# Expert 0's first two inner chunks in pieces of 192 and 96 tokens, and 28 stand-ins behind a branch, in a fused attention and mixture-of-experts kernel

## The chip, the cores and the metric

The kernel runs on one core of a Trainium2 chip. The metric is the device time of one execution in microseconds (us), the median of the runs made. A core has five engines that work side by side, each through its own queue in order: TensorE (PE in the profile, PEld for its weight loads), VectorE (DVE), ScalarE (ACT), GpSimd (POOL) and SyncE (SP, which here only issues DMAs).

## The reference

Attention over a window of 128 keys with a bias by distance, for 4 batches, 8 heads and 576 positions of width 64; then a first layer of 8 experts, to which the 2304 tokens are dealt out by the order of their gate logits, 288 to each; then a dense second layer. Cut to the two layers:

```python
flat = (x @ w_gate).flatten()
order = np.argsort(-flat)               # tokens to experts, 288 at most for each
...
for e in range(E):
    mask = assigned == e
    h = np.maximum(x[mask] @ w1[e], 0.0)   # 288 x 512 by 512 x 1024
    out[mask] = h @ w2[e]
...
h = x @ w_in
return (h * (1.0 / (1.0 + np.exp(-h)))) @ w_out
```

## The kernel before

Four stages follow one another on the core: attention tile by tile (to some 120 us), the routing that turns logits into a list of tokens for each expert (to 140 us), the first layer expert by expert (`moe1`, to some 370 us), and the second layer in groups of 512 tokens (`moe2`, to the end). Products of float32 are made as three matmuls of rounded parts: each operand x is split into a high part `xh` (a cast) and the rest `xl` (a subtraction), and hi*xh, lo*xh and hi*xl are summed in PSUM. Weights are split in the same way (`Weights.fetch`: a DMA into `raw`, a cast on ScalarE, line 728, and a subtraction on VectorE, line 729). Three weights of the first layer are split during attention, in `split_early`; the others follow on the run.

Between routing and the first layer stands a branch (line 1024): if the fast routing did not deal out all tokens properly, a slow one is run. With these inputs it is not taken into that code. Ahead of it, `gather0` (line 1021) has POOL issue three indirect DMAs that fetch expert 0's 288 tokens as three tiles of 96 into `xg0`, which lies in a buffer of the weights' ring. Behind it TensorE runs stand-ins (`k.busy`, line 440: matmuls on constants whose result is not read; here 256 columns each, into the PSUM tile `pd`), as many as the first number of `BUSY_G` says.

`gather(e)` in `moe1` makes `xh` and `xl` of an expert: for each tile of 96 tokens four transposes on TensorE (line 836) into PSUM, a cast on ScalarE (line 843) and a subtraction on VectorE (line 844). For expert 0 further stand-ins come behind the transposes of each tile, and the third tile goes through two PSUM tiles (`y2`, `y3`) in two halves. For the other experts POOL issues the gathers (line 825).

`first(e, f)` makes chunk f (128 of 1024 inner columns) of an expert: 12 matmuls (line 859) of 128x128 by 128x288, then the ReLU's high part on ScalarE (line 862) and its rest on VectorE (line 863). `second(e, f)` adds 12 further matmuls (lines 758 to 760). For each chunk the loop calls `first`, then `fetch` of the weight four chunks ahead, and `second` two chunks later. The order of instructions within an engine is chosen by a planner from estimated times, but not between those marked with `keep_in_program_order`: these stay in the order of the program. An engine's queue is served in its order, so an instruction that waits holds all behind it.

The PSUM pool `ph` has two buffers: `pd` takes one, and chunks' results `p` take turns. `px` (two) holds the transposes of a tile, `py` the four sums of `second`.

Of the kernel before, what the change touches and what calls it, by code (L numbers as in the profile page):

```python
# [8 lines left out]
F32 = mybir.dt.float32  # L9
F32R = mybir.dt.float32r  # L10
# [4 lines left out]
ALU = mybir.AluOpType  # L15
# [4 lines left out]
P = 128  # L20
B, H, S, D = 4, 8, 576, 64
# [3 lines left out]
CAP = N // E  # L25
# [367 lines left out]
JR = 96  # L393
JT = N // JR
PER = CAP // JR
# [288 lines left out]
DC = 4  # L684
# [72 lines left out]
def three(nc, out, whi, wlo, xhi, xlo, start, stop):  # L757
    nc.tensor.matmul(out, whi, xhi, start=start, stop=False)  # L758
    nc.tensor.matmul(out, whi, xlo, start=False, stop=False)  # L759
    nc.tensor.matmul(out, wlo, xhi, start=False, stop=stop)  # L760
# [5 lines left out]

SOON = 7
LATE = (0, 1, 2, 4, 5, 7, 8, 10, 11)
BUSY_G = (12, 4, 4, 3)


def load_group(tc, pool, yd, g, width=BT):

    o, n = GROUPS[g]
    r = pool.tile([P, DC, width], F32, name="yr", bufs=1)
    tc.nc.sync.dma_start(r[:, :, :n], yd.rearrange("c p n -> p c n")[:, :, o:o + n])
    return r


def split_group(tc, pool, r, g, y=None, cols=range(DC)):  # L780
    o, n = GROUPS[g]
    yh, yl = y or (pool.tile([P, DC, BT], F32R, name=x, bufs=1)[:, :, :n] for x in ("yh", "yl"))
    for c in cols:
        i = tc.nc.scalar.copy(yh[:, c], r[:, c, :n])
        j = tc.nc.vector.tensor_tensor(yl[:, c], r[:, c, :n], yh[:, c], ALU.subtract)
        if len(cols) < DC:
            tc.keep_in_program_order(i)
            tc.keep_in_program_order(j)
    return yh, yl


def moe(tc, wts, xtab, xg0, idx96, k, yd, yg, by128, idx128, out):
    nc = tc.nc
    with tc.tile_pool(name="ph", bufs=2, space=PSUM) as ph, tc.tile_pool(name="py", bufs=1, space=PSUM) as py, \
            tc.tile_pool(name="px", bufs=2, space=PSUM) as px:
        y0, p0 = moe1(tc, wts, xtab, xg0, idx96, k, yd, yg, by128, ph, py, px)
        moe2(tc, wts, yd, yg, y0, p0, idx128, out, ph, py, px)


def part0(tc, wts, p, yh, yl, f):  # L800

    hi, lo = wts.ready[E * FC1 + f]
    for dc in range(DC):
        w = slice(dc * P, dc * P + P)
        three(tc.nc, p, hi[:, w], lo[:, w], yh[:, dc, :], yl[:, dc, :], dc == 0, dc == DC - 1)


def moe1(tc, wts, xtab, xg0, idx96, k, yd, yg, by128, ph, py, px):

    nc = tc.nc  # L810
    with tc.tile_pool(name="m1", bufs=2) as m1:
        xs = {}
        ident = k.ident
        pd = ph.tile([P, CAP], F32, name="p")
        k.busy(tc, pd, BUSY_G[0], 2)

        def gather(e):
            xh = m1.tile([P, DC, CAP], F32R, name="xh")
            xl = m1.tile([P, DC, CAP], F32R, name="xl")
            for j in range(PER):  # L820
                if e == 0:
                    xg = xg0[0:JR, j]
                else:
                    xg = m1.tile([JR, H * D], F32, name="xg", bufs=3)
                    nc.gpsimd.indirect_dma_start(xg, None, xtab,
                                                 bass.IndirectOffsetOnAxis(ap=idx96[:, e * PER + j:e * PER + j + 1], axis=0))
                halves = (slice(0, 2), slice(2, 4)) if e == 0 and j == PER - 1 else (slice(0, 4),)
                pts = []
                for i, d in enumerate(halves):
                    if len(halves) == 1:  # L830
                        pt = px.tile([P, DC, JR], F32, name="pt")
                    else:
                        pt = py.tile([P, 512], F32, name=f"y{2 + i}")[:, 0:DC * JR].rearrange("p (a b) -> p a b", b=JR)
                    pts.append(pt)
                    for dc in range(d.start, d.stop):
                        tr = nc.tensor.transpose(pt[:, dc, :], xg[:, dc * P:dc * P + P], ident[0:JR, 0:JR])  # L836
                        if e < 2:
                            tc.keep_in_program_order(tr)
                if e == 0:
                    k.busy(tc, pd, BUSY_G[j + 1], 2)  # L840
                for d, pt in zip(halves, pts):
                    c = slice(j * JR, (j + 1) * JR)
                    x = nc.scalar.copy(xh[:, d, c], pt[:, d])  # L843
                    y = nc.vector.tensor_tensor(xl[:, d, c], pt[:, d], xh[:, d, c], ALU.subtract)
                    if e == 0:
                        tc.keep_in_program_order(x)
                        tc.keep_in_program_order(y)
            xs[e] = (xh, xl)

        def first(e, f):  # L850
            xh, xl = xs[e]
            hi, lo = wts.ready[e * FC1 + f]
            p = ph.tile([P, CAP], F32, name="p")

            steps = [(w, x, dc) for w, x in ((hi, xh), (lo, xh), (hi, xl)) for dc in range(DC)]
            if e + f == 0:
                steps = [(w, xh, dc) for dc in range(DC) for w in (hi, lo)] + steps[8:]
            for i, (w, x, dc) in enumerate(steps):
                nc.tensor.matmul(p, w[:, dc * P:dc * P + P], x[:, dc, :], start=(i == 0), stop=(i == 11))  # L859
            hh = m1.tile([P, CAP], F32R, name="hh", bufs=3)  # L860
            hl = m1.tile([P, CAP], F32R, name="hl", bufs=3)
            nc.scalar.activation(hh, p, AF.Relu)
            nc.vector.scalar_tensor_tensor(hl, p, 0.0, hh, ALU.max, ALU.subtract)
            return hh, hl

        ys = {}

        def second(e, f, h):
            hh, hl = h
            hi, lo = wts.ready.pop(e * FC1 + f)  # L870
            if f == 0:
                ys[e] = [py.tile([P, 512], F32, name=f"y{d}")[:, 0:CAP] for d in range(DC)]
            for d in range(DC):
                w = slice(512 + d * P, 512 + d * P + P)
                three(nc, ys[e][d], hi[:, w], lo[:, w], hh, hl, f == 0, f == FC1 - 1)
            if f == FC1 - 1:
                yo = m1.tile([P, DC, CAP], F32, name="yo", bufs=1)
                for d in range(DC):
                    nc.scalar.copy(yo[:, d], ys[e][d])
                nc.sync.dma_start(yd.rearrange("c p n -> p c n")[:, :, e * CAP:(e + 1) * CAP], yo)  # L880

        gather(0)
        wts.fetch(5)
        pend, y0 = [], None
        for e in range(E):
            for f in range(FC1):
                n = e * FC1 + f
                h = first(e, f)
                wts.fetch(n + 4)
                if n % 9 == 4 and n // 9 < SOON:  # L890
                    wts.fetch64(n // 9, wts.keep)
                if f == 3 and e == 2:
                    by128(px.tile([P, 3, JT // 4], F32, name="pt"))
                if f == 1 and e + 1 < E:
                    gather(e + 1)
                pend.append((e, f, h))
                if len(pend) > 2:
                    second(*pend.pop(0))
                if e == E - 1 and f == 1:
                    r0 = load_group(tc, yg, yd, 0)  # L900
                if e == E - 1 and 2 < f < 7:
                    y0 = split_group(tc, yg, r0, 0, y0, (f - 3,))
        second(*pend.pop(0))
        p0 = px.tile([P, BT], F32, name="pt")
        part0(tc, wts, p0, *y0, 0)
        second(*pend.pop(0))
    return y0, p0
# [177 lines left out]
```

## Time and profile before

| | us |
|---|---|
| timed runs | 760.45, 762.08, 762.80 (median 762.08) |
| profiled execution | 764.28 |
| its span, from the first to the last instruction | 762.5 |
| TensorE busy in the span | 745.0 |
| VectorE, ScalarE, POOL busy | 423.5, 328.9, 120.7 |
| granted TensorE clock, mean | 0.994 |

The profiled execution is one execution by itself, 1.5 to 3.8 us longer than the timed ones. All times of rows are counted from the start of its span. A granted clock of 1.00 is 2.4 GHz, 0.50 is 1.2 GHz. Busy time of matmuls is modelled from their starts, and matmuls overlap, so that the distance from start to start tells their pace.

### The profile page before, as it was taken

How to read it: one execution, taken by the hardware profiler on the slowest of the kernel's cores; microseconds unless marked ns; L12 is line 12 of the kernel's file. 1: busy time of each engine (PE TensorE's matmuls, PEld its weight loads, DVE VectorE, ACT ScalarE, POOL GpSimd, SP SyncE). 2: the span in 40 equal slices, each digit the busy share in tenths (PEclk: the TensorE clock that was granted, in tenths of full speed). 3: DMA queues.
4: the chain of work that ended last, by engine and by line, in shares of the span. 5: the costliest groups of instructions: out<-in, count | busy, mean ns of one | idle time of the engine just before them, and what ended most of it. 6: DMA issues, size and time to landing. Idle time of an engine off the chain costs nothing.

```text
span 762.5 us, 14997 instructions
## 1 busy us (share of the span) xinstructions
PE 745.0 (98%) x5927; PEld 643.4 (84%) x5927; DVE 423.5 (56%) x1092; ACT 328.9 (43%) x667; POOL 120.7 (16%) x180
## 2 busy tenths in 40 slices
PE   8999999799999999999999999999999999999996
PEld 4887874599999999999888888888888888888895
DVE  5888886557748758757499953223322232222331
ACT  4666661256655656654456532213221232121332
POOL 2866871211101101000000002000100001000101
PEclk9999999899999999999999999999999999999999
DMA  8999870258688778664634211000100001000100
GB/s 224 258 278 275 265 215 29 65 176 271 194 288 280 209 236 271 197 212 126 230 129 158 84 56 55 1 1 0 70 15 0 1 1 55 1 1 0 42 15 28
DMA packets 45257, 95.58 MB, mean 125 GB/s; under 512 B 4576, under 2 KB 19072, under 8 KB 45184
## 3 DMA queue, kind: packets, MB, share of 16 engines
q1 hardware_dynamic: 41984, 84.88, 36.0%
q0 software_dynamic: 3040, 9.46, 3.8%
q8 instruction: 47, 0.77, 0.4%
q10 hardware_dynamic: 160, 0.26, 0.1%
q14 instruction: 26, 0.21, 0.1%
HBM read 80.43 MB, written 14.16 MB: 124 GB/s over the span
## 4 chain that ended last, share of the span: by engine, by line
PE 74%; DMA 3%; DVE 2%; ACT 1%; issue 0%; POOLq 0%; SPq 0%; ACTq 0%
PE y L922 25%; PE p L859 12%; PE pt L758 4%; PE pt L759 4%; PE p L759 4%; PE p L758 4%; PE pt L760 4%; PE p L760 4%; PE y L758 4%; PE y L759 4%; PE y L760 4%; DMA raw<-w 2%; PE pt L836 1%; DVE w L729 1%; DMA yd<-yo 1%; DMA w<-xtab,idx 1%
## 5 line engine op out<-in xcount | busy, mean ns | idle before, releaser
L922 PE MATMUL y<-w,gh 128*128 128x512 f32 x548 | 180.4, 389 | 0.0
L922 PEld LDWEIGHTS y<-w,gh 128*128 128x128 f32 x548 | 102.2, 188 | 20.5
L922 PE MATMUL y<-w,gl 128*128 128x512 f32 x274 | 106.7, 389 | 0.0
L729 DVE TENSOR_TENSOR w<-raw,w 128x1024 fp32r<-128x1024 f32 x61 | 74.6, 1225 | 53.1 <-ACT w L728 53.0
L934 POOL DMA_INDIRECT out<-raw,idx x18 | 18.2, 1013 | 448.0 <-ACT raw L932 416.9
L728 ACT CAST w<-raw 128x1024 fp32r<-128x1024 f32 x61 | 63.9, 1050 | 43.9 <-PE y L760 24.3
L859 PE MATMUL p<-xh,w 128*128 128x288 f32 x512 | 81.9, 299 | 0.9 <-ACT xh L843 0.9
L966 DVE TENSOR_TENSOR s<-pt,s 128x512 f32<-128x512 f32 (+1 forms) x40 | 25.5, 637 | 92.5 <-ACT s L965 92.5
L759 PE MATMUL y<-hl,w 128*128 128x288 f32 x256 | 74.9, 296 | 0.0
L760 PE MATMUL y<-hh,w 128*128 128x288 f32 x256 | 74.7, 295 | 0.0
L859 PEld LDWEIGHTS p<-xh,w 128*128 128x128 f32 x512 | 73.2, 192 | 1.7 <-ACT xh L843 1.4
L976 DVE TENSOR_TENSOR gl<-s,gh 128x512 fp32r<-128x512 f32 (+1 forms) x73 | 48.0, 658 | 44.6 <-ACT gh L975 44.6
L758 PE MATMUL y<-hh,w 128*128 128x288 f32 x256 | 71.2, 298 | 0.0
L966 DVE TENSOR_TENSOR s<-p,s 128x512 f32<-128x512 f32 (+1 forms) x40 | 25.5, 637 | 82.2 <-ACT s L965 82.2
L975 ACT CAST gh<-s 128x512 fp32r<-128x512 f32 (+1 forms) x73 | 43.4, 595 | 59.8 <-DVE s L966 45.4
L965 ACT ACTIVATE s<-pt 128x512 f32<-128x512 f32 (+1 forms) x40 | 22.2, 556 | 94.0 <-PE pt L760 81.9
L965 ACT ACTIVATE s<-p 128x512 f32<-128x512 f32 (+1 forms) x40 | 22.2, 556 | 90.7 <-PE p L760 81.6
L922 PEld LDWEIGHTS y<-w,gl 128*128 128x128 f32 x274 | 51.4, 188 | 10.6
L758 PE MATMUL pt<-yh,w 128*128 128x512 f32 (+1 forms) x160 | 58.9, 369 | 0.2 <-DVE s L966 0.2
L223 ACT ACTIVATE pe<-sc,mx 128x128 f32<-128x128 f32 x144 | 49.4, 394 | 22.2 <-DVE mx L231 22.1
L759 PE MATMUL pt<-yl,w 128*128 128x512 f32 (+1 forms) x160 | 58.8, 368 | 0.0
L758 PE MATMUL p<-yh,w 128*128 128x512 f32 (+1 forms) x160 | 58.8, 368 | 0.0
(191 smaller groups left out, 1466.7 us busy)
## 6 DMA issues: line engine op xcount, KB each, us to landing
raw<-w SPq DMA_DIRECT2D x96, 512.0 KB, 4.2
va<-vA SPq DMA_DIRECT2D x18, 292.0 KB, 4.6
ks<-kT SPq DMA_DIRECT2D x36, 128.0 KB, 6.3
vt<-vT SPq DMA_DIRECT2D x18, 256.0 KB
xtab<-xt SPq DMA_DIRECT2D x18, 256.0 KB, 4.2
yd<-yo SPq DMA_DIRECT2D x8, 576.0 KB
qs<-qT SPq DMA_DIRECT2D x34, 128.0 KB, 4.5
yr<-yd SPq DMA_DIRECT2D x4, 1024.0 KB, 5.2
```

The source lines that it names most:

```text
L223: keep(nc.scalar.activation(pe[:, c, :], sc[:, c, :], AF.Exp, bias=mx[:, c:c + 1], scale=-1.0))
L728: x = nc.scalar.copy(hi, r)
L729: y = nc.vector.tensor_tensor(lo, r, hi, ALU.subtract)
L758: nc.tensor.matmul(out, whi, xhi, start=start, stop=False)
L759: nc.tensor.matmul(out, whi, xlo, start=False, stop=False)
L760: nc.tensor.matmul(out, wlo, xhi, start=False, stop=stop)
L859: nc.tensor.matmul(p, w[:, dc * P:dc * P + P], x[:, dc, :], start=(i == 0), stop=(i == 11))
L922: mm = nc.tensor.matmul(a, x[:, w], y[:, 512:], start=(f + i == 0), stop=(f == FC2 - 1 and i == 2))
L965: nc.scalar.activation(s, p, AF.Sigmoid)
L966: nc.vector.tensor_tensor(s, p, s, ALU.mult)
L975: nc.scalar.copy(gh, s)
L976: nc.vector.tensor_tensor(gl, s, gh, ALU.subtract)
```

## The change

Expert 0's tokens are no longer prepared by `gather(0)` but by a new function `opening`. It goes through the first two tiles (`turn(0)`, `turn(1)`), then makes chunk 0's 12 matmuls on these 192 tokens (`piece(0, ps[0], a)`), then does the third tile (`turn(2)`), whose casts are now made on VectorE, and then chunk 1's 12 matmuls on 192 tokens. `first(0, 0)` and `first(0, 1)` add the 96 tokens that are left. All of this is kept in the order of the program. The stand-ins are 28 behind the branch, 2 behind the first tile, 4 behind the second and none behind the third, where they were 12, 4, 4 and 3. The fetch ahead of the loop goes up to weight 3 instead of weight 4; the loop's own call for chunk 1 then fetches weight 4. The order of the three products in chunk 0 is now that of all other chunks.

```diff
-BUSY_G = (12, 4, 4, 3)
+BUSY_G = (28, 2, 4)
...
+        def opening():
+            keep = tc.keep_in_program_order
+            xh = m1.tile([P, DC, CAP], F32R, name="xh")
+            xl = m1.tile([P, DC, CAP], F32R, name="xl")
+            xs[0] = (xh, xl)
+
+            def turn(j):
+                c = slice(j * JR, (j + 1) * JR)
+                if j < PER - 1:
+                    parts = [(slice(0, DC), px.tile([P, DC, JR], F32, name="pt"))]
+                else:
+                    parts = [(slice(2 * i, 2 * i + 2), py.tile([P, 512], F32, name=f"y{2 + i}")[:, 0:DC * JR].rearrange("p (a b) -> p a b", b=JR))
+                             for i in range(2)]
+                for d, pt in parts:
+                    for dc in range(d.start, d.stop):
+                        keep(nc.tensor.transpose(pt[:, dc, :], xg0[0:JR, j, dc * P:dc * P + P], ident[0:JR, 0:JR]))
+                if j < PER - 1:
+                    k.busy(tc, pd, BUSY_G[j + 1], 2)
+                for d, pt in parts:
+                    keep((nc.scalar.copy if j < PER - 1 else nc.vector.tensor_copy)(xh[:, d, c], pt[:, d]))
+                for d, pt in parts:
+                    keep(nc.vector.tensor_tensor(xl[:, d, c], pt[:, d], xh[:, d, c], ALU.subtract))
+
+            def piece(f, p, c):
+                hi, lo = wts.ready[f]
+                steps = [(w, x, dc) for w, x in ((hi, xh), (lo, xh), (hi, xl)) for dc in range(DC)]
+                for i, (w, x, dc) in enumerate(steps):
+                    keep(nc.tensor.matmul(p[:, c], w[:, dc * P:dc * P + P], x[:, dc, c], start=(i == 0), stop=(i == 11)))
+
+            turn(0)
+            turn(1)
+            a, b = slice(0, 2 * JR), slice(2 * JR, CAP)
+            ps = [ph.tile([P, CAP], F32, name="p") for f in range(2)]
+            piece(0, ps[0], a)
+            turn(2)
+            piece(1, ps[1], a)
+            return piece, ps, b
...
         def first(e, f):
             xh, xl = xs[e]
             hi, lo = wts.ready[e * FC1 + f]
-            p = ph.tile([P, CAP], F32, name="p")
-            steps = [(w, x, dc) for w, x in ((hi, xh), (lo, xh), (hi, xl)) for dc in range(DC)]
-            if e + f == 0:
-                steps = [(w, xh, dc) for dc in range(DC) for w in (hi, lo)] + steps[8:]
-            for i, (w, x, dc) in enumerate(steps):
-                nc.tensor.matmul(p, w[:, dc * P:dc * P + P], x[:, dc, :], start=(i == 0), stop=(i == 11))
+            if e == 0 and f < 2:
+                p = ps[f]
+                piece(f, p, rest)
+            else:
+                p = ph.tile([P, CAP], F32, name="p")
+                steps = [(w, x, dc) for w, x in ((hi, xh), (lo, xh), (hi, xl)) for dc in range(DC)]
+                for i, (w, x, dc) in enumerate(steps):
+                    nc.tensor.matmul(p, w[:, dc * P:dc * P + P], x[:, dc, :], start=(i == 0), stop=(i == 11))
...
-        gather(0)
-        wts.fetch(5)
+        piece, ps, rest = opening()
+        wts.fetch(4)
```

`gather` keeps what it does for the other experts and loses its branches for expert 0.

## Rows read from the trace of the kernel before

**Rows 1.** The page: busy time; granted clock in 40 slices; the chain's shares.
```profile
PE 745.0 (98%) x5927; PEld 643.4 (84%) x5927; DVE 423.5 (56%) x1092; ACT 328.9 (43%) x667; POOL 120.7 (16%) x180
...
PEclk9999999899999999999999999999999999999999
...
PE 74%; DMA 3%; DVE 2%; ACT 1%; issue 0%; POOLq 0%; SPq 0%; ACTq 0%
```

**Rows 2.** Coarse windows: stretch, length, busy PE, PEld, DVE, ACT, POOL, clock, DMA.
```profile
160.00:200.00 40.00, 40.00 (x307) 40.00 (x307) 27.36 (x42) 22.42 (x37) 2.76 (x3) 1.00 0.70 214
...
360.00:370.00 10.00, 10.00 (x57) 8.84 (x56) 0.97 (x2) 2.92 (x7) 0.00 (x0) 1.00 0.98 363
```

**Rows 3.** Waits of PE from 150 us on: us in total, times, longest.
```profile
PE pt L758 <- DVE s L966: 0.2, 1, 0.2
```

**Rows 4.** Windows of 1 us around the opening of expert 0.
```profile
143.00:144.00 1.00, 0.00 (x0) 0.00 (x0) 0.00 (x0) 0.00 (x0) 0.76 (x1) 1.00 0.70 180
...
145.00:146.00 1.00, 1.00 (x9) 0.97 (x8) 0.36 (x1) 0.48 (x1) 0.71 (x1) 0.64 0.62 164
...
151.00:152.00 1.00, 1.00 (x6) 1.00 (x6) 1.00 (x2) 0.19 (x1) 0.00 (x0) 0.50 0.00 0
152.00:153.00 1.00, 1.00 (x9) 1.00 (x9) 0.64 (x1) 0.00 (x0) 0.00 (x0) 0.95 0.58 86
```

**Rows 5.** The chain that ended last: start, length, what ran.
```profile
144.42 0.55 PE pt L836 x4
...
145.42 0.64 PE pt L836 x4
...
147.55 1.23 PE p L440 x3
...
149.13 4.78 PE p L859 x24
153.91 0.66 PE pt L836 x8
...
167.66 1.58 PE p L859 x12
...
376.50 2.72 PE y L922 x12
```

**Rows 6.** TensorE's timeline: start, length, line, tile, count, idle time ahead.
```profile
141.04 1.48 PE L440 MATMUL p<-ones 128*128 128x256 bf16 x12 [0.47 <-DVEq L1024]
144.42 0.55 PE L836 MATMUL pt<-cst,w 96*128 96x96 f32 x4 [1.90 <-DMA w<-xtab,idx]
...
145.25 0.81 PE L836 MATMUL pt<-cst,w 96*128 96x96 f32 x4
...
146.70 0.85 PE L836 MATMUL y<-cst,w 96*128 96x96 f32 x4
...
153.75 0.82 PE L836 MATMUL pt<-cst,xg 96*128 96x96 f32 x8
```

**Rows 7.** ScalarE's timeline in the same stretch.
```profile
145.13 0.48 ACT L843 CAST xh<-pt 128x384 fp32r<-128x384 f32 x1 [6.07 <-PE pt L836]
146.09 0.48 ACT L843 CAST xh<-pt 128x384 fp32r<-128x384 f32 x1 [0.48 <-PE pt L836]
148.76 0.54 ACT L843 CAST xh<-y 128x192 fp32r<-128x192 f32 x2 [2.19 <-PE p L440]
149.18 2.00 ACT L728 CAST w<-raw 128x1024 fp32r<-128x1024 f32 x2
...
157.06 0.66 ACT L750 ACTIVATE f<-raw 128x512 f32<-128x512 f32 x1
```

**Rows 8.** VectorE: the third tile's subtractions (ns min/median/max), and the weights' splits.
```profile
L844 DVE TENSOR_TENSOR xl<-y,xh x2: 347/352/357, 149.1 to 149.4; 128x192 fp32r<-128x192 f32 x2
...
150.27 2.36 DVE L729 TENSOR_TENSOR w<-raw,w 128x1024 fp32r<-128x1024 f32 x2 [0.54 <-ACT w L728]
```

**Rows 9.** SP's queue: the loads behind the first split weights.
```profile
152.66 0.33 SPq L742 DMA_DIRECT2D raw<-w  x1
```

More of the change, by code (lines that the diff above doesn't have):

```diff
@@ L820, in gather @@
             for j in range(PER):
[L821 to L847, printed above, removed]
+                xg = m1.tile([JR, H * D], F32, name="xg", bufs=3)
+                nc.gpsimd.indirect_dma_start(xg, None, xtab,
+                                             bass.IndirectOffsetOnAxis(ap=idx96[:, e * PER + j:e * PER + j + 1], axis=0))
+                pt = px.tile([P, DC, JR], F32, name="pt")
+                for dc in range(DC):
+                    tr = nc.tensor.transpose(pt[:, dc, :], xg[:, dc * P:dc * P + P], ident[0:JR, 0:JR])
+                    if e < 2:
+                        tc.keep_in_program_order(tr)
+                c = slice(j * JR, (j + 1) * JR)
+                nc.scalar.copy(xh[:, :, c], pt)
+                nc.vector.tensor_tensor(xl[:, :, c], pt, xh[:, :, c], ALU.subtract)
             xs[e] = (xh, xl)
```

## The prediction

> **What bounds the kernel now.** I read the page first: TensorE is busy for 98% of the span and makes up most of the chain that ended last, so only time in which TensorE waits or runs slowly can be won [rows 1]. Next come the coarse windows: from 160 us on TensorE is busy through whole stretches of both layers, with the granted clock at 1.00 [rows 2], and after 150 us its only recorded wait is 0.2 us, at the start of layer two [rows 3]. So whatever the opening of expert 0 wins or loses goes whole into the end time, and nothing later takes it back by itself.
>
> The windows of 1 us show that opening. Between 143 and 144 us TensorE does nothing; within 145 to 146 the granted clock falls from 1.00 (2.4 GHz) to 0.50 (1.2 GHz), and it comes back in 152 to 153 [rows 4]. A share of 0.64 in that first microsecond puts the fall near 145.28, the 0.95 puts the rise near 152.1: 6.8 us at half speed, the only slice of the page that shows less than nine tenths [rows 1]. Ahead of the fall the engine had run its 12 stand-ins from 141.04 and then sat idle for 1.90 us, until the first gather landed [rows 6]. The chain gives the order of that stretch: gather, transposes and stand-ins, ScalarE's cast, then 24 matmuls of chunks 0 and 1 [rows 5].
>
> One wait there isn't explained. The third tile's transposes end at 147.55 in the chain, yet ScalarE's casts of it start at 148.76 [rows 5, 7]: 1.2 us in which only three stand-ins are shown. For tiles one and two the cast follows the transposes at once [rows 5, 7].
>
> **The change part by part.** I follow TensorE from the branch (141.04) to the first instruction behind chunks 0 and 1, the transposes of expert 1, which start at 153.75 [rows 6].
>
> *28 stand-ins instead of 12.* The 12 start within 1.48 us, the last of them some 0.27 ahead of that end, so 1.21 / 11 = 0.11 each [rows 6]. The last of 28 starts at 141.04 + 27 x 0.11 = 144.01 and ends at 144.28. The gather's landing releases the transposes at 144.42 [rows 6], so the 16 added ones (1.76 us) lie in the wait and cost nothing. Were the gather to land 0.5 us sooner, they would cost that 0.5. What they are worth is the clock: with the idle 1.90 us cut to about 0.15 I take it to stay at 1.00. Nothing in the trace fell to 0.50 after so short a gap.
>
> *First tile, second tile.* Transposes at the high clock go eight in 0.66, or 0.083 each [rows 5]: tile one's four run from 144.42 to 144.75. Two stand-ins (0.22) follow, then the second tile's transposes, whose gather was there by 145.25 [rows 6]: they are done by about 145.6. ScalarE casts tile one 145.13 to 145.61, then tile two 145.61 to 146.09 (0.48 each) [rows 7]. The four stand-ins behind it are over by then. So the first real matmul starts at 146.13 instead of 149.13 [rows 5]: it no longer waits for the third tile. That is **3.00 us**, of which 1.2 is the unexplained wait.
>
> *Narrower matmuls.* Twelve of 288 columns take 1.58, twelve of 512 take 2.72 [rows 5]: 0.132 and 0.227 each, a slope of 0.42 ns a column and 11 ns on top. For 192 columns that gives 0.092. For 96 it gives 0.052, but each still loads a weight of 128 columns, and the nearest row, the transposes with the same load and the same 96 columns, goes at 0.083; I take 0.08, with 0.052 and, as the upper end, the 0.132 of the wide ones. So 24 x 0.092 + 24 x 0.08 = 2.21 + 1.92 = 4.13, where 24 wide ones at the high clock would be 3.17. The split alone costs 0.96 us of TensorE (0.28 at the low bound, 3.17 if no narrow matmul beats the wide pace).
>
> The Trainium skill (page "TensorE: Matmul & The Clock Gate", section "LDWEIGHTS (loading the stationary operand)") gives a load as its columns over 1.2 GHz, 107 ns for 128 by my estimate. By it the 48 matmuls would be 5.1 us and the opening 1.0 us longer. The trace disagrees: the transposes' loads go through at 0.083 [rows 5].
>
> *Third tile, now behind chunk 0's first piece.* Piece 146.13 to 147.23; four transposes to 147.56 (the third gather was there by 146.70 at the latest [rows 6], so no wait); chunk 1's first piece to 148.67. Meanwhile VectorE makes both casts and both subtractions. Its subtraction of this shape from PSUM is 0.35 [rows 8]; a copy there isn't shown. Below it lie ScalarE's casts of that shape, two in 0.54 [rows 7], above it a whole weight's split, two in 2.36 [rows 8]: 0.27 to 1.18, of which I take 0.35, the nearest in engine and shape. 147.6 + 2 x 0.35 = 148.3 for the casts, ahead of 148.67, and 149.0 for the subtractions, which are read from the ninth of the 96-column matmuls on, at 149.3. At 1.18 a copy TensorE would lose some 1.4; at 0.5 nothing. Chunks 0 and 1 end with 24 x 0.08: **150.59**. That is 3.16 us ahead of 153.75. Of these, 3.00 is the earlier start; the rest is 4.62 (149.13 to 153.75) against 0.33 + 4.13.
>
> *One weight fetch moved behind chunk 1.* ScalarE's 1.0 and VectorE's 1.2 for weight 4 (half of two in 2.00 and two in 2.36) stood behind the third tile, under matmuls [rows 7, 8]. Now they go between the ReLUs of chunks 1 and 2; the weight is read by chunk 4, some 8 us later, so nothing waits for it. Queued behind VectorE's split are the load on SP at 152.66, and behind that load ScalarE's square at 157.06 with the next weight's cast [rows 7, 9]. POOL's gathers and their order stay.
>
> **How the numbers follow.** In the profiled execution's terms (764.28, span 762.5 and 1.78 around it) the forecast is 764.28 - 3.16 = 761.1. But the three timed runs lie 1.48, 2.20 and 3.83 below it. I read this so: the 1.2 us wait is of the profiled execution, since no timed run comes within 1.2 of it; and the fastest, 760.45, is a run without the low clock. For the median then: 762.08 - (3.16 - 1.2) = 760.1. From the other side: without fall and wait the unchanged kernel would start its 24 wide matmuls no later than third transposes 146.70 + 0.33 + 0.2 of latency + 0.35 cast = 147.6 at most, and be done by 150.7, about where the changed one is; so the changed kernel should take what the fastest run took, 760.45, give or take 0.6. I forecast **760.4 us**, 0.2% less. A measurement of this kernel can tell about 0.3% (2.3 us) from no change.
>
> **The rivals.**
> - *The gain is whole.* If the 1.2 us wait and the fall are in the timed runs too, it is 762.08 - 3.16 = 758.9. For it: the profile shows both; against it: the spread of the timed runs.
> - *Weight loads set the pace.* At 0.132 for each of the 48 (the wide pace, under which loads of this size are known to fit) the pieces cost 6.34 instead of 4.13: 762.6. Against it: the transposes' pace. By the rule of the Trainium skill above it would be 761.4.
> - *The clock falls all the same.* The transposes and a short second idle stretch (145.7 to 146.13, until the cast) follow the stand-ins. If it falls near 145.3 and is back at 152.1, as now, everything doubles: tile two cast by 146.4, first piece (12 x 0.185) to 148.6, transposes at 0.16 to 149.3, second piece to 151.5, then 4 narrow ones to 152.1 and 20 at 0.08 to 153.7. That is no sooner than now, and without the 1.2 us wait to win: 762.08 + 1.2 - 0.05 = 763.2, slower than before. It decides from a fall ahead of about 149; later than that little is left to slow. For it: the transposes and stand-ins that ran from 145.25 on did not lift the clock before the matmuls had run for some 3 us [rows 4 to 6]; against it: TensorE's idle time ahead of 145.3 is a tenth of what it was.
> - *ScalarE's queue stalls behind a load.* The SP load of 152.66 waits for the second split, which moves to about 153.5, while TensorE is 3.2 us further; the square behind it waits until 158, and the ReLU of chunk 3 behind that, if the order stays: 1 to 2 us lost, 762.
> - *The median run has no fall.* Then the change brings nothing but its narrower matmuls: 762.1 to 762.6.
>
> **Chances.** Forecast (759.6 to 761.2) 0.50; whole gain 0.18; loads 0.08; fall 0.10; queue 0.06; no fall in the median 0.08. The range 758.8 to 762.8 leaves out the fall and the lower half of the whole gain. Faster by over 0.3% (below 759.8): the whole gain and a sixth of the forecast's share, 0.26. Slower by over 0.3% (above 764.4): half of the fall, 0.05. Between: 0.69.
>
> **What would show it.** In the changed profile: a granted clock of 1.00 from 144 to 154; no idle stretch over 0.5 us on TensorE after 141; twelve 192-column matmuls from about 146.1, in 1.1 us; twelve of 96 in 0.6 to 1.0; expert 1's transposes near 150.6; casts of the third tile on VectorE done ahead of chunk 1's first piece. Wrong would be a fall of the clock, a start of the first piece behind 147, or a TensorE wait between 150 and 165 for ScalarE or a weight.

## The result and the profile after

| | before | after |
|---|---|---|
| median of six runs each | 762.65 us (760.45 to 764.64) | 770.49 us (767.08 to 774.59) |
| profiled execution | 764.28 us | 769.55 us |
| its span, mean granted clock | 762.5 us, 0.994 | 767.8 us, 0.995 |

The ratio is 1.0107 with a 95% interval of 1.0079 to 1.0135: the change makes the kernel 1.1% slower, where 0.2% faster was forecast. A second timing gave 1.0077 (1.0044 to 1.0111); its slowest execution, 778.01 us, which is also the profiled one, is a slow run and left out of that ratio.

The loss lies in the opening of expert 0, and the timeline of TensorE after the change shows it (columns as in [rows 6], which it answers to):

```profile
141.88 3.23 PE L440 MATMUL p<-ones 128*128 128x256 bf16 x28 [0.46 <-DVEq L1048]
145.12 0.55 PE L833 MATMUL pt<-cst,w 96*128 96x96 f32 x4
...
145.73 0.53 PE L833 MATMUL pt<-cst,w 96*128 96x96 f32 x4
146.09 0.60 PE L440 MATMUL p<-ones 128*128 128x256 bf16 x4
150.30 2.02 PE L845 MATMUL p<-xh,w 128*128 128x192 f32 x8 [3.61 <-ACT xh L837]
...
152.97 0.84 PE L833 MATMUL y<-cst,w 96*128 96x96 f32 x4
...
158.58 0.86 PE L865 MATMUL pt<-cst,xg 96*128 96x96 f32 x8
```

The 28 stand-ins run right up to the first tile's transposes, as planned, and no time is lost ahead of them. Both early tiles are transposed by 146.3. Then TensorE has nothing to do for 3.61 us, because ScalarE's casts are late. ScalarE's timeline in the same stretch answers to [rows 7]:

```profile
148.41 0.48 ACT L837 CAST xh<-pt 128x384 fp32r<-128x384 f32 x1 [8.51 <-remote]
149.77 0.48 ACT L837 CAST xh<-pt 128x384 fp32r<-128x384 f32 x1 [0.88 <-remote]
```

ScalarE sat idle for 8.51 us ahead of the first of them, though the transposes that it reads ended at 145.67 (145.12 + 0.55). It is 2.74 us late; the second is 3.51 us late (149.77 against 146.26). The releaser is given as "remote": the profile finds no local instruction that ended at that moment. The chain that ended last says the same in its own words (start, length, what; it answers to [rows 5]):

```profile
141.83 6.44 another core or an unknown queue
148.27 0.03 ACTq L837
...
148.41 0.48 ACT xh L837
148.89 0.85 another core or an unknown queue
...
149.77 0.49 ACT xh L837
...
150.30 2.87 PE p L845 x12
```

The trace's own record of TensorE's semaphore update for tile one (the signal that ScalarE waits for) stands at 148.27, not at 145.67, and that for tile two at 149.75. In this profile and in that of every other kernel below, ScalarE's first cast starts 0.14 us behind that record: where the cast is late, the signal is late, and ScalarE adds nothing. The windows of 1 us (columns as in [rows 4]) show the second half of the loss:

```profile
147.00:148.00 1.00, 0.00 (x0) 0.00 (x0) 0.00 (x0) 0.00 (x0) 0.69 (x2) 1.00 0.55 152
148.00:149.00 1.00, 0.00 (x0) 0.00 (x0) 0.08 (x1) 0.48 (x1) 0.28 (x1) 0.93 0.45 152
149.00:150.00 1.00, 0.00 (x0) 0.00 (x0) 0.48 (x1) 0.23 (x1) 0.00 (x0) 0.50 0.62 180
...
155.00:156.00 1.00, 1.00 (x8) 1.00 (x8) 0.87 (x1) 0.00 (x0) 0.00 (x0) 0.66 0.00 0
156.00:157.00 1.00, 1.00 (x11) 1.00 (x11) 0.00 (x0) 0.00 (x0) 0.00 (x0) 1.00 0.27 33
```

In the long wait the granted clock falls from 1.00 (2.4 GHz) to 0.50 (1.2 GHz), by the share of 0.93 near 148.86, and is back near 155.7 (0.66). It is as long a fall as before (6.8 us), but 5.4 us of it now lie under the real matmuls (150.30 to 155.68), where it was 3.0 (149.13 to 152.1).

The sum, counted from TensorE's first stand-in to the first instruction behind chunks 0 and 1: before 153.75 - 141.04 = 12.71 us, after 158.58 - 141.88 = 16.70. That is +3.99 of the 5.3 us between the two profiled executions; the branch itself is reached 0.84 later (141.88 against 141.04), and 0.4 is spread over the rest. What did POOL do meanwhile? Its timeline shows expert 1's three gathers, issued at once behind expert 0's:

```profile
144.91 0.92 POOL L861 DMA_INDIRECT xg<-xtab,idx  x1 [0.30 <-issue]
146.13 0.92 POOL L861 DMA_INDIRECT xg<-xtab,idx  x1 [0.30 <-issue]
147.36 0.92 POOL L861 DMA_INDIRECT xg<-xtab,idx  x1 [0.30 <-issue]
```

They cover 144.91 to 148.28, and the first cast starts 0.13 us after the last of them. That nearness is no rule: in the experiments below the late cast stands between 0.01 us ahead of the end of POOL's last issue (e4_fed) and 1.73 behind it (e5_small). The gathers stand there in the kernel before too, where they cover 144.1 to 147.4; there it is the third tile's cast, 1.2 us late, that the prediction left as an unexplained wait.

### The profile page after: what moved, and what is told of

The parts are those of the page before. It is cut to its first block, busy times and chain, and to the rows that moved or that the text cites. A ratio compares the mean times of both kernels' runs of the same rounds, so it can differ in the third digit from the quotient of the medians.

```text
span 767.8 us, 15068 instructions
## 1 busy us (share of the span) xinstructions
PE 749.4 (98%) x5962; PEld 647.5 (84%) x5962; DVE 424.6 (55%) x1094; ACT 329.0 (43%) x665; POOL 122.2 (16%) x180
## 4 chain that ended last, share of the span: by engine, by line
PE 75%; DMA 2%; DVE 1%; another core or an unknown queue 1%; ACT 1%; issue 0%; POOLq 0%; SPq 0%; ACTq 0%
PE y L946 25%; PE p L883 12%; PE pt L758 4%; PE pt L759 4%; PE p L759 4%; PE p L758 4%; PE pt L760 4%; PE p L760 4%; PE y L758 4%; PE y L759 4%; PE y L760 4%; DMA raw<-w 1%; PE p L845 1%; PE pt L865 1%; DMA yd<-yo 1%
## 5 line engine op out<-in xcount | busy, mean ns | idle before, releaser
L883 PE MATMUL p<-xh,w 128*128 128x288 f32 x496 | 77.9, 295 | 0.0
L883 PEld LDWEIGHTS p<-xh,w 128*128 128x128 f32 x496 | 69.7, 188 | 0.2
L758 PE MATMUL pt<-yh,w 128*128 128x512 f32 (+1 forms) x160 | 58.9, 369 | 0.6 <-DVE s L990 0.5
L760 PE MATMUL pt<-yh,w 128*128 128x512 f32 (+1 forms) x160 | 58.8, 368 | 0.0
```

## The experiments

Three theories were set against each other. **A:** the gathers of expert 1, issued by POOL, hold back the release of expert 0's transposes to ScalarE. **B:** the longer run of stand-ins on TensorE does it. **C:** the narrow pieces, with their own order on the engines, do it. A fourth came with the clock: TensorE runs out of work behind the second tile, and the rest follows.

All runs stand in this table; each was profiled in one execution. "Late" is the time from the end of tile one's transposes on TensorE's timeline to the start of its cast on ScalarE's; "opening" runs from the first stand-in to the first instruction behind chunks 0 and 1. Ratios are to the kernel before on the same chip, with 95% intervals.

| kernel | stand-ins | POOL behind expert 0's gathers | late | opening | median us, ratio |
|---|---|---|---|---|---|
| before | 12 | three gathers | 0.16 (third tile 1.21) | 12.71 | 763.6 (59 runs) |
| after | 28 | three gathers | 2.74 | 16.70 | 770.49, 1.0107 (1.0079 to 1.0135) |
| e1_standins | 28 | three gathers | 3.14 | 11.78 | 765.45, 1.0032 (1.0006 to 1.0058) |
| e2_pieces | 12 | three gathers | 0.16 | 12.42 | 764.29, 1.0017 (0.9983 to 1.0051) |
| e3_held | 28 | gathers held | 0.16 | 10.76 | 765.20, 1.0020 (0.9990 to 1.0049) |
| e4_fed | 28 | three gathers | 2.67 | 14.02 | 766.13, one run |
| e5_small | 28 | three small gathers | 3.93 | 16.68 | 769.12, one run |
| e6_loads | 28 | nothing (loads on ScalarE) | 0.16 | 11.86 | 765.65, one run |
| e7_pieces_held | 28 | gathers held | 0.16 | 10.98 | 762.84, 0.9988 (0.9964 to 1.0013) |
| e8_plain_held | 28 | gathers held | 0.16 | 9.26 | 761.40, 0.9963 (0.9938 to 0.9988) |
| e9_hold12 | 12 | gathers held | 0.16 | 9.54 | 761.53, 0.9980 (0.9952 to 1.0008) |
| e10_after_again | 28 | three gathers | 2.63 | 19.19 | 768.94, 1.0077 (1.0044 to 1.0111) |
| e11_pool_loads | 28 | three plain loads | 0.16 | 10.78 | 764.55, one run |
| e12_pool_work | 28 | three copies, no DMA | 0.16 | 10.80 | 760.82, one run |

**The stand-ins alone.** The kernel before with 28 stand-ins and nothing else.

```diff
-BUSY_G = (12, 4, 4, 3)
+BUSY_G = (28, 4, 4, 3)
```

> The kernel before with 28 stand-ins instead of 12 behind the branch, nothing else. Theory A (expert 1's gathers, which POOL issues and the DMA engines carry at that time, hold back the release of expert 0's transposes): the first cast starts 0.7 us behind the start of its transposes as in the kernel before, the third again 1 to 2 us late; the clock stays at 1.00 and the time is 760 to 762. Theory B (a long run of stand-ins right ahead of the transposes holds their release back): the first cast comes some 3.3 us behind the start of its transposes, as in the changed kernel, and the time is 765 or more. Theory C (the narrow pieces queued behind the transposes do it): as A, 760 to 762, and no cast is late by over 1.5 us.

The first cast on ScalarE's timeline, then the first real matmul on TensorE's:

```profile
148.89 0.48 ACT L843 CAST xh<-pt 128x384 fp32r<-128x384 f32 x1 [9.09 <-DMA xg<-xtab,idx]
```

```profile
150.29 2.39 PE L859 MATMUL p<-xh,w 128*128 128x288 f32 x16 [2.66 <-ACT xh L843]
...
153.57 0.82 PE L836 MATMUL pt<-cst,xg 96*128 96x96 f32 x8
```

Tile one's transposes ended at 145.75 (145.20 + 0.55), so its cast is 3.14 late without any narrow piece: theory C falls. Theory A by itself had this cast on time, as before, and 760 to 762; the late cast and the 765.45 are what B expected. The clock did not fall in this profile, although TensorE idled for 2.66 us.

**The pieces alone.** The changed kernel with 12 stand-ins.

```diff
-BUSY_G = (28, 2, 4)
+BUSY_G = (12, 2, 4)
```

> The changed kernel with 12 stand-ins behind the branch instead of 28; the pieces stay. Theory A: the casts are late again, by 2 to 4 us from the start of their transposes, and the time stays near 770. Theory B: the first cast comes 0.7 us behind the start of its transposes; the clock falls near 145 as in the kernel before, and the time is 763 to 766. Theory C: as A, near 770.

```profile
144.12 0.91 ACT L837 CAST xh<-pt 128x384 fp32r<-128x384 f32 x2 [6.08 <-PE pt L833]
```

```profile
145.08 1.93 PE L845 MATMUL p<-xh,w 128*128 128x192 f32 x8
```

ScalarE's casts are on time, and the first piece starts 1.67 us behind the transposes (143.41), as forecast. So the stand-ins have a part in it, as B says, and the pieces none; A had expected late casts and a time near 770. The clock still fell, for 3.4 us.

**Expert 1's gathers held.** The changed kernel, with POOL made to wait for expert 0's third tile ahead of expert 1's first gather.

```diff
+                if e == 1 and j == 0:
+                    held = m1.tile([1, 1], F32, name="held", bufs=1)
+                    tc.keep_in_program_order(nc.gpsimd.tensor_copy(held, xs[0][1][0:1, DC - 1, CAP - 1:CAP].bitcast(F32)))
-                nc.gpsimd.indirect_dma_start(xg, None, xtab,
+                g = nc.gpsimd.indirect_dma_start(xg, None, xtab,
...
+                if e == 1:
+                    tc.keep_in_program_order(g)
```

> The changed kernel with expert 1's three gathers held back on POOL until the third tile of expert 0 has been split. Theory A: the casts of tiles one and two follow their transposes within 0.9 us of the start, the first piece starts near 146.1, the clock stays at 1.00, and the time is 760 to 763. Theories B and C: the casts are as late as in the changed kernel (3 us and more), the clock falls, and the time stays near 770.

ScalarE's first casts, and the place on TensorE's timeline where the hold is paid for:

```profile
145.30 0.91 ACT L837 CAST xh<-pt 128x384 fp32r<-128x384 f32 x2 [6.04 <-PE pt L833]
```

```profile
155.03 0.55 PE L870 MATMUL pt<-cst,xg 96*128 96x96 f32 x4 [1.48 <-DMA xg<-xtab,idx]
```

With the same 28 stand-ins the cast is 0.16 behind its transposes and the clock stays at 1.00 through the opening, which is 5.9 us shorter than after the change (10.76 against 16.70). This is what theory A expects, and by B the casts would still be late. So neither theory holds alone: tile one's cast is late with the 28 stand-ins and the three gathers together, on time with either taken away. The time, 765.20, misses A's 760 to 763 and is that of before. The gathers now land too late for their own place in the order, and TensorE waits 1.48 us for the first of them.

**TensorE fed through the wait.** The changed kernel with 24 stand-ins behind the second tile instead of 4.

```diff
-BUSY_G = (28, 2, 4)
+BUSY_G = (28, 4, 24)
```

> The changed kernel with 4 and 24 stand-ins behind the first and second tile instead of 2 and 4, so that TensorE has work behind the transposes for 2.6 us more. If the release of a transpose comes late only where TensorE runs out of work behind it, the casts of tiles one and two now start within 0.9 us of their transposes' start, and the first piece behind the stand-ins, near 148.5. By theories A and B the casts stay 2 to 4 us late and the first piece starts at 150 or later.

```profile
147.32 0.48 ACT L837 CAST xh<-pt 128x384 fp32r<-128x384 f32 x1 [8.37 <-remote]
```

TensorE's transposes ended at 144.65, so the cast is as late as after the change (2.67 against 2.74), with TensorE at work up to it; that it ran out of work was not the cause. What the extra stand-ins do is to keep the clock at 1.00: the opening takes 14.02 instead of 16.70. From the first matmul to the end of chunk 1 it needs 5.74 us (149.21 to 154.95) where the changed kernel needs 8.28 (150.30 to 158.58): 2.54 us of that opening hang on the clock.

**Hold, and a later place for expert 1.** As in the held version above, with the hold on the third tile's first cast, and with expert 1's gathers and transposes given out behind chunk 4 rather than chunk 1.

```diff
-                if f == 1 and e + 1 < E:
+                if f == (1 if e else 4) and e + 1 < E:
```

> The changed kernel with expert 1's gathers held on POOL until the third tile's first cast, and their transposes placed behind chunk 4. By theory A no cast is late, the clock stays at 1.00 over the opening, the last narrow matmul starts 11.5 us behind the issue of the first gather (17.4 in the changed kernel, 13.4 for the last wide one in the kernel before), TensorE doesn't wait for expert 1's gathers, and the time is 760 to 762. By the other theories nothing is won over the first held kernel: 764 to 766.

TensorE's timeline, with the change's pieces at the high clock and no wait between them:

```profile
144.38 0.55 PE L833 MATMUL pt<-cst,w 96*128 96x96 f32 x4 [0.34 <-DMA w<-xtab,idx]
...
146.05 1.14 PE L845 MATMUL p<-xh,w 128*128 128x192 f32 x8
...
147.48 0.49 PE L833 MATMUL y<-cst,w 96*128 96x96 f32 x4
147.75 1.12 PE L845 MATMUL p<-xh,w 128*128 128x192 f32 x8
...
149.16 1.01 PE L845 MATMUL p<-xh,w 128*128 128x96 f32 x8
...
150.45 1.06 PE L845 MATMUL p<-xh,w 128*128 128x96 f32 x8
...
151.79 0.76 PE L758 MATMUL y<-hh,w 128*128 128x288 f32 x4
```

This is the opening that the prediction had in mind: first matmul 1.67 us behind the first transposes. And yet the time, 762.84, is not told from that of before, and misses the 760 to 762 expected. The rows show what eats the gain: each set of twelve of 192 columns takes 1.41 to 1.43 (147.75 to 149.16), each of 96 takes 1.29 to 1.34 (149.16 to 150.45): 0.118 and 0.110 for one.

**Hold without the pieces.** The kernel before with 28 stand-ins, the same hold and the same later place.

> The kernel before with 28 stand-ins and with expert 1's gathers held in the same way, without pieces. By theory A no cast is late, the 24 wide matmuls start about 6.9 us behind the issue of the first gather and the last of them at 10.0, where it is 13.4 in the kernel before; the time is 759 to 761, no worse than with the pieces. By theories B and C the casts are late as with 28 stand-ins alone, and the time is 763 to 766.

ScalarE's casts, then TensorE's wide matmuls:

```profile
146.55 0.48 ACT L848 CAST xh<-pt 128x384 fp32r<-128x384 f32 x1 [5.87 <-PE pt L841]
147.20 0.48 ACT L848 CAST xh<-pt 128x384 fp32r<-128x384 f32 x1 [0.17 <-PE pt L841]
147.90 0.54 ACT L848 CAST xh<-y 128x192 fp32r<-128x192 f32 x2 [0.22 <-PE y L841]
```

```profile
148.27 2.36 PE L864 MATMUL p<-xh,w 128*128 128x288 f32 x16
...
151.92 0.79 PE L758 MATMUL y<-hh,w 128*128 128x288 f32 x4 [0.24 <-ACT hh L867]
```

All three tiles are cast as soon as they are transposed, and the whole opening takes 9.26 us, 3.45 less than before. The median is 761.40, just above the 759 to 761 expected and 0.4% below the kernel before (the interval lies wholly below 1); as the changed kernel stands 0.8 to 1.1% above that, this version beats both. Beside the pieces under the same hold it starts its first matmul 0.76 later (2.43 against 1.67 behind the transposes) and needs 2.09 less from there (3.65 against 5.74).

**Hold with 12 stand-ins.** To part the hold from the stand-ins.

```diff
-BUSY_G = (28, 4, 4, 3)
+BUSY_G = (12, 4, 4, 3)
```

> The kernel before with its 12 stand-ins and expert 1's gathers held on POOL until the third tile's first cast and given to POOL at chunk 4: the hold without the longer run of stand-ins. Theory A (expert 1's gathers, issued by POOL, hold back the release of expert 0's transposes): the third tile's cast follows its transposes within 0.5 us instead of the 1.2 to 1.5 of before, the casts stand near 4.9, 5.9 and 7.1 us behind the first gather's issue. If the clock is a matter of the idle time ahead of the transposes alone, it still falls to 0.50 within the opening, as the 12 leave some 1.9 us idle, and the last opening matmul is at 11.5 to 12.5 rather than 13.4: 761.5 to 763.5, between before and the version with 28. Rival (the stand-ins bring nothing): clock and last matmul as with 28, 9.6, and the same time.

```profile
143.60 0.55 PE L841 MATMUL pt<-cst,w 96*128 96x96 f32 x4 [2.03 <-DMA w<-xtab,idx]
...
149.63 0.79 PE L758 MATMUL y<-hh,w 128*128 128x288 f32 x4 [0.24 <-issue]
```

The third tile's cast is on time, and the opening takes 9.54 us. In this execution the clock did not fall, though TensorE had idled for 2.03 us, more than the 1.90 of [rows 6]. That, and a median of 761.53 beside 761.40, is what the rival expected: a gain in time from 28 stand-ins instead of 12 under the hold is not shown. Over all executions the granted clock seems better kept with 28: its mean over the span was 0.997 or more in 18 of 20 timed executions of the two versions with 28 stand-ins and the later place, in 7 of 10 with 28 and the hold alone, in 4 of 10 with 12 held, in 28 of 59 of the kernel before, and in 1 of 12 of the changed kernel. (The profile with one whole fall of 6.8 us has a mean of 0.994; one with a fall of 3.4 us has 0.997, and e11_pool_loads has 0.996 without any fall from 138 to 170 us, so the mean is a rough sign.)

**Data or issue?** Two versions of the pieces under hold, with something else in the old place of expert 1's gathers. In one, three gathers of 16 rows instead of 96, into a tile that nothing reads:

```diff
+        few = m1.tile([16, PER, H * D], F32, name="few", bufs=1)
+        for j in range(PER):
+            tc.keep_in_program_order(nc.gpsimd.indirect_dma_start(few[:, j], None, xtab,
+                                     bass.IndirectOffsetOnAxis(ap=idx96[0:16, PER + j:PER + j + 1], axis=0)))
```

> The changed kernel with expert 1's gathers held back behind the third tile's cast, and in their old place three gathers of 16 rows instead of 96 into a tile that nobody reads: as many issues on POOL, a sixth of the data. If the issue on POOL (or the count of DMAs that land) holds back the release of the transposes, the first cast starts 3 us behind the start of its transposes again. If it is the data on its way, the first cast starts 0.7 us behind them, or late by well under 1 us.

In the other, three plain loads of 96 rows, issued by ScalarE behind the first cast:

```diff
             turn(0)
+            same = m1.tile([JR, PER, H * D], F32, name="same", bufs=1)
+            for j in range(PER):
+                keep(nc.scalar.dma_start(same[:, j], xtab[j * JR:(j + 1) * JR, :]))
```

> The same kernel with, in place of the small gathers, three plain loads of as many bytes as the old gathers, issued by ScalarE between its casts of tiles one and two. The second cast comes up to 1 us later, for the issues stand ahead of it. If any DMA traffic of this size holds back the release, the third tile's casts start over 1 us behind the start of their transposes; if only gathers issued by POOL do, they start 0.4 us behind it, as they do with the gathers held.

A small gather takes POOL nearly as long as a large one, and with a sixth of the bytes TensorE waits longest of all. POOL's timeline, then TensorE's:

```profile
143.72 0.86 POOL L913 DMA_INDIRECT few<-xtab,idx  x1 [0.30 <-issue]
```

```profile
149.52 2.02 PE L845 MATMUL p<-xh,w 128*128 128x192 f32 x8 [3.86 <-ACT xh L837]
```

With all the bytes and no gather behind expert 0's, the second cast waits only for ScalarE's own three issues ahead of it (145.64 to 146.96), which is why this run's opening is 0.9 longer than without them. The first cast says nothing of the loads, as they are issued behind it. The third tile does: its cast, on VectorE, starts 0.37 behind the start of its transposes, as expected with no release held. ScalarE's rows, TensorE's third tile and VectorE's cast of it:

```profile
145.62 0.48 ACT L837 CAST xh<-pt 128x384 fp32r<-128x384 f32 x1 [6.19 <-PE pt L833]
145.64 1.32 ACTq L850 DMA_DIRECT2D same<-xtab  x3
```

```profile
148.95 0.49 PE L833 MATMUL y<-cst,w 96*128 96x96 f32 x4
```

```profile
149.32 0.62 DVE L837 CAST xh<-y 128x192 fp32r<-128x192 f32 x2 [1.25 <-PE y L833]
```

It is the small gathers that decide: with a sixth of the bytes the release is late all the same, so it is not the bytes. **Which issue on POOL?** Again the pieces under hold, with plain loads on POOL in that place, or with copies.

```diff
+            tc.keep_in_program_order(nc.gpsimd.dma_start(same[:, j], xtab[j * JR:(j + 1) * JR, :]))
```

> The pieces with expert 1's gathers held, as in the version before, plus three plain loads of 96 rows of 2 KB each into a tile that nothing reads, issued by POOL in the place where expert 1's gathers stood. If any DMA that POOL issues holds back the release of TensorE's transposes, the casts of tiles one and two stand at 7 to 9 us behind the first gather's issue instead of 5.1 and 5.5, TensorE waits 2 us or more for the first cast, and the run is 766 to 770 us. If it is the indirect form alone (a list of rows that POOL turns into addresses), the casts stand at 5.1 and 5.5 and the run takes 761 to 765 us.

```diff
+            tc.keep_in_program_order(nc.gpsimd.tensor_copy(work, wts.ready[0][0][0:JR].bitcast(F32)))
```

> The same with three copies of 96 x 1024 elements on POOL in that place and no DMA. If whatever POOL executes in that stretch holds back the release, the casts are late again, 7 us or more; if it is the issue of DMAs, they stand at 5.1 and 5.5 and the run takes 761 to 765 us.

For each, POOL's timeline and ScalarE's, the loads first:

```profile
144.60 1.61 POOL L913 DMA_DIRECT2D same<-xtab  x3
```

```profile
145.76 1.09 ACT L837 CAST xh<-pt 128x384 fp32r<-128x384 f32 x2 [5.88 <-PE pt L833]
```

```profile
142.03 3.25 POOL L913 COPY work<-w 96x1024 f32<-96x1024 f32 x3
```

```profile
143.40 0.91 ACT L837 CAST xh<-pt 128x384 fp32r<-128x384 f32 x2 [6.08 <-PE pt L833]
```

Both casts start in the middle of POOL's work and 0.16 us behind their transposes. In one execution each, neither three plain loads from POOL nor three microseconds of POOL's own work held the release, where three indirect DMAs did in every execution profiled with 28 stand-ins.

**The changed kernel again.**

> The changed kernel, unaltered, beside the kernel before on this chip. Its loss in the first timing (7.8 us in the median) is larger than what its profiled opening shows (5.3). If the late release has a length of its own in every execution, the ratio is again 1.006 to 1.014, and this profile's casts of tile one stand anywhere between 5 and 9 us behind the first gather's issue; if the first profile was typical, tile one's cast is again within 0.5 of 7.4.

The late release is there again: tile one's cast stands 7.26 us behind the first gather's issue (7.36 in the first profile). The spread of this kernel goes with the clock: of its twelve timed executions the four longest (772.68 to 778.01) have a mean granted clock of 0.988 or 0.989, the other eight (766.11 to 770.88) 0.993 to 0.997. In this execution the fall lasted 17.1 us, from 150.3 on (the windows give 0.51 for 150 to 160 and 0.54 for 160 to 168), instead of 6.8, and it took 778.01 us.

## Why the prediction was wrong

From the first stand-in the prediction gave the opening 150.59 - 141.04 = 9.55 us; it took 16.70. That is 7.15 of the 8.4 us between the 761.1 that it gave in the profiled execution's terms and the 769.55 measured. By its steps:

- *28 stand-ins cost nothing* held only ahead of the transposes. There they fill the wait for the first gather, which ended 0.14 us sooner behind the first stand-in than before (145.12 - 141.88 = 3.24 against 3.38). Behind the transposes they had a price that the prediction put at nothing: with the pieces the opening took 16.70 with 28 and 12.42 with 12, and 28 stand-ins alone made the kernel before 0.3% slower.
- *What the stand-ins are worth* held only with the gathers out of the way: then the clock stayed at 1.00 through the opening in all profiles with 28. In the changed kernel they moved the idle stretch rather than removing it: 1.90 us ahead of the transposes became 3.61 behind them.
- **The step that failed: "for tiles one and two the cast follows the transposes at once", kept for the changed kernel.** The forecast put the first real matmul 1.71 us behind the first transposes; it came 5.18 behind (150.30 - 145.12). That is 3.47 of the 7.15 us missed. The trace of before held the warning, the third tile's cast 1.2 us behind its transposes [rows 5, 7]. I named it and then laid it to the profiled execution, since no timed run came within 1.2 us of it. Three more runs of the kernel before took 762.51, 763.57 and 764.64, the last longer than the profiled 764.28, so that reason fell too. The wait is there with the gathers of expert 1 and gone without them; with the 28 stand-ins, which the change itself brought, it moved to tile one and grew to 2.6 us and more.
- *Narrower matmuls* were mis-sized. Forecast 0.092 and 0.08, 4.13 for the 48; measured at the high clock 0.118 and 0.110, 1.43 + 1.41 + 1.29 + 1.34 = 5.47. The 24 wide ones took 3.28 at the high clock (e1_standins, 150.29 to 153.57, 0.137 each), so the split costs 2.2 us, not 0.96. I had taken the pace of the transposes for the 96-column pieces, and it doesn't carry over. The rule of the Trainium skill that the prediction set aside (page "TensorE: Matmul & The Clock Gate", section "LDWEIGHTS (loading the stationary operand)": 107 ns for 128 columns, an estimate by its formula) came out nearer: by it, 5.1.
- *The clock falls all the same* was the rival that came true in kind, not in its mechanism: not the stretches ahead of the casts but a wait of 3.61 us brought the fall, and it began near 148.86. Behind the first stand-in that is 148.02 in the times of the kernel before, ahead of the 149 that the prediction named as the point from which little is left. As the matmuls had been put off as well, much was left: the pieces took 8.28 us where the same at 1.00 took 5.74. That is 2.54 us; with 1.34 of narrower matmuls and 3.47 of wait, less the 0.14 and some hundredths, it is the 7.15.
- *VectorE's copies* held: 0.34 each for a forecast of 0.35, by its timeline after the change.

```profile
153.53 0.68 DVE L837 CAST xh<-y 128x192 fp32r<-128x192 f32 x2 [2.69 <-PE y L833]
```

- *The moved work* held. The fetch of weight 4, and ScalarE's queue behind it, cost nothing: TensorE's list of waits from 140 to 180 us (total, times, longest) holds, behind the branch, the 3.6 us for the cast and no weight:

```profile
PE p L845 <- ACT xh L837: 3.6, 1, 3.6
```

The medians lie 7.8 and 5.5 us apart (770.49 less 762.65, 768.94 less 763.44), the profiled executions 5.3. That the rest of the first distance is the clock fits the counts above (a mean clock of 0.997 or more in 28 of 59 executions of before and in 1 of 12 of the changed kernel), but it wasn't taken apart run by run.

What stays open is how indirect DMAs on POOL hold the release. Nor does the trace tell whether only the signal came late or the transposes themselves ended late: ends of matmuls are modelled from their starts, and the semaphore update is the first thing on record behind them. It is not enough that one is being issued: with 12 stand-ins and the pieces the first two casts were on time (144.12) under gathers from 143.04 on, and under hold the first ReLU of the pieces starts at 150.65, at once behind its matmuls, with a gather on POOL from 149.10 to 150.94. Late releases were seen only where three further indirect DMAs followed expert 0's three without a break; why 28 stand-ins make the first release late and 12 only the third tile's isn't known. Nor were expert 0's own gathers tried in another form.

## What to carry to other kernels

Where an engine's recorded start lags the end of its producer and the releaser reads "remote" or an unknown queue, look at what POOL issues in that stretch: a run of indirect DMAs for later work, put out as early as possible, can go with a late release of the step that the end time waits for, and a one-element copy on POOL that reads the urgent result is a cheap way to hold them. A wait of a microsecond that the trace shows and the argument can't place should be kept in the sum, and asked after on the other tiles, rather than put down to the one execution. And pieces cut to start a matmul sooner have to be priced at the pace of real matmuls of that width: here a third of the columns took four fifths of the time.

## What the runs showed of the hardware

- Three indirect DMAs on POOL, of 0.92 us each (0.86 for a sixth of the rows), went with casts of tile one 2.6 to 3.9 us behind the end of its transposes in all five profiles with 28 stand-ins ahead, and 0.16 behind in both with 12. With 28, three plain loads issued by POOL (1.61 us for the three) and three copies on POOL (3.25 us) went with 0.16.
- From TensorE's semaphore update on record to the start of ScalarE's first cast it was 0.14 us in all fourteen profiles, late or not (148.27 to 148.41 after the change).
- Whether another engine's release can be held is not shown. One was on time while gathers were being issued: with the pieces and 12 stand-ins the cast of ScalarE released the first piece within 0.05 us (cast until 145.03, matmul at 145.08); but there TensorE's releases were on time too.
- The clock fell after 1.90 us of idle time in one execution and stayed at 1.00 through 2.03 and 2.66 us in others, so the length of the idle stretch alone doesn't tell whether it falls.
- A matmul with a weight of 128 columns took 0.110 us for 96 columns, 0.118 for 192 and 0.132 to 0.140 for 288, while transposes with a load of the same width went at 0.083 [rows 5].
